# q and k of blocks 6 to 11 turned by transposing transfers instead of TensorE products and ScalarE copies

## The chip, the cores and the metric

The kernel runs on one core of a Trainium2 chip. The metric is the device time of one launch in microseconds, lower is better. Times are of whole launches; a profile is of one launch, recorded by the hardware profiler.

A core has engines that run their own instruction lists in order and wait for each other by semaphores: TensorE (PE in the profile, its weight loads PEld), VectorE (DVE), ScalarE (ACT), GpSimd (POOL) and SyncE (SP). Here GpSimd and SyncE do nothing but issue transfers (DMAs), GpSimd the loads and SyncE the stores. The transfers themselves run on 16 DMA engines that all queues share.

## The reference

Two parts, one behind the other. The first is a recurrence over 768 tokens for 4 batches x 8 heads of 64 dimensions; the second is a channel mix with three matrices.

```python
for t in range(S):                      # per batch and head
    state = gamma * state + outer(k[t], v[t])
    x[t]  = scale * q[t] @ state        # gamma = 1 - 2**(-5-head)
xk = mu_k * x + (1 - mu_k) * x_prev     # x: 4 x 768 x 512, x_prev: one token earlier
xr = mu_r * x + (1 - mu_r) * x_prev
k  = relu(xk @ w_k)                     # 512 x 1024
out = sigmoid(xr @ w_r) * (k * k @ w_v) # 512 x 512, 1024 x 512
```

## The kernel before

The 4 x 768 tokens are cut into 12 blocks of 256 tokens, three to a batch, numbered 0 to 11; a block is two chunks of 128 tokens. The recurrence is done in chunks: scores of k against q inside a chunk, masked by the causal order, times v, plus q times a state that is carried from chunk to chunk. Blocks 6 to 11 (`HALF`) work in four chunks of 64 tokens, so their products are 64x64 on quarters of TensorE's array; blocks 1 to 5 (`WIDE`) use chunks of 128.

There is no scheduler. One list of words, `ORDER` (lines 23 to 74), is walked once, and each word emits its instructions; so each engine's order is the order of its words in that list. A word is a code, a block and further indices; `@` names the PSUM banks that it writes and `~` the engine (v VectorE, a ScalarE, p GpSimd, s SyncE). The words that matter here, for a block n:

- `lq`, `lk`, `lv` (`load`, line 222): GpSimd loads q, k and v. q and k are cast from float32 to float16 on the way, into `Q16` and `K16`, rings of four buffers each. k goes in two transfers, one for each half of the block's 256 tokens (line 230). q goes in one (line 235), with tokens 2p and 2p+1 side by side in partition p.
- `Tq`, `Tk` (`trans`, line 264): TensorE turns q and k, tokens in partitions, into dimensions in partitions, by products with the identity into PSUM; for blocks 6 to 11 these are 32 products of 64x64 each (line 278).
- `Eq`, `Ek` (`turned_q`, `turned_k`): ScalarE copies the turned q and k from PSUM to `QT` and `KT`, rings of three buffers. The copy of q also puts its tokens back into plain order.
- `S` (`scores`, `scores_half`, line 318): TensorE multiplies `KT` with `QT`; `M` (`masked`, line 347): VectorE masks the scores into float16.
- `C`, `U`, `G`: the new state, its sum on VectorE (line 419) and its decay.
- `I` and `J` (`inter`, line 441): TensorE multiplies q with the carried state; `Y` (`intra`, line 462): masked scores with v; `D` (`yout`, line 507): VectorE scales the result into `xT`. For blocks 6 to 11 `Y` ends with the second half of `inter`.
- `dx`, `X` (lines 529 and 538, VectorE): the two mixes xk and xr. `K` (lines 552 and 562), `R` (592) and `V` (604) are TensorE's large products with w_k, w_r and w_v; `Qa`, `Qb` and `s` are ScalarE's relu, square and sigmoid; `O` (line 610, VectorE) multiplies gate and value into `OS`, a ring of four buffers; `st` (line 617) stores it from SyncE.
- `z`: products of zeros that keep TensorE busy early on.

Heads are handled in four pairs, one head in each half of the 128 partitions. `HEADS = ((0, 1), (3, 2), (4, 5), (7, 6))` is the order within the pairs: in two of the four the higher head comes first. `heads(j)` gives for each head of pair j its half `a`, its number and the half `hp` of its output. With this order `inter`, whose products read half `a` and write half `hp`, uses all four 64x64 quarters of the array in turn.

Every transfer has a semaphore out of a ring of eight for GpSimd and of eight for SyncE and ScalarE together, and waits for the transfer that used it last. SyncE's list before is two early loads and 24 stores, each waiting for its `O`.

Of the kernel before, what the change touches and what calls it, by code (L numbers as in the profile page):

```python
# [21 lines left out]
HEADS = ((0, 1), (3, 2), (4, 5), (7, 6))  # L22
ORDER = """
lk.0.0.2~s gy.0 lq.0.2.4~p lv.0~p lq.0.0.2~s lk.0.2.4~p ck.0.0.2~a z.12@6 Tk.0.0.2@0 mu Tq.0.2.4@1
cq.0.0.2~a z.2@6 Tq.0.0.2@2 Ek.0.0.2~a vs.0~v mt@3 Eq.0.0.2~a z.2@6 S.0.1.0.2@45 S.0.0.0.2@67
M.0.0.0.2~v Eq.0.2.4~a M.0.1.0.2~v Tk.0.2.4@2 Ek.0.2.4~a C.0@01 U.0.0~a U.0.1 S.0.0.2.4@67
M.0.0.2.4~v I.0@45 S.0.1.2.4@01 me M.0.1.2.4~v lv.1~p vs.1~v gy.1~a G.0~a z.4@2 Y.0 D.0~v lk.1~p
Tk.1@0 Ek.1~a C.1@67 U.1.0 lq.1~p z.1@2 Tq.1@1 Eq.1~a dx.0~v X.0.0.0 z.4@2 S.1.1@01 lk.2~p I.1@45
S.1.0@23 M.1.1~v M.1.0~v lq.2~p Tq.2@6 Eq.2~a wk.1~p X.0.0.3 Tk.2@0 X.0.0.2 z.1@1 Y.1 J.1 X.0.0.1
D.1~v U.1.1 Ek.2~a z.1@2 S.2.1@01 S.2.0@23 K.0.2@6 dx.1~v K.0.3@4 Qa.0.3 Qa.0.2 wk.0~p z.2@5  # L30
K.0.1@7 Qa.0.1 K.0.0@5 Qb.0.2 X.0.1.0 X.1.0.2 lv.2~p Qa.0.0 Qb.0.1 X.1.0.3 wr~p X.1.0.1 X.1.0.0
K.1.2@4 lv.3~p G.1~a K.1.1@7 X.0.1.1 vs.2~v Qa.1.2 Qb.1.2 M.2.1~v Qb.0.0 C.2@5 U.2.0 K.1.0@6
lq.3~p Qa.1.1 X.0.1.2 X.0.1.3 K.1.3@0 Qa.1.3 I.2@45 R.0.1@1 R.0.0@7 s.0.1 M.2.0~v Y.2 Qa.1.0
X.1.1.3 X.1.1.2 Qb.1.0 Tq.3@1 Eq.3~a J.2 X.1.1.0 X.1.1.1 R.1.0@6 s.0.0 lk.3~p Tk.3@1 vs.3~v D.2~v
dx.2~v X.2.0.2 X.2.0.0 C.3@23 X.2.0.3 Ek.3~a s.1.0 X.2.0.1 lk.4~p U.3.0~a R.1.1@0 lq.4~p s.1.1
Tk.4@1 S.3.1@45 S.3.0@67 Qb.1.1 Qb.1.3 U.3.1 lv.4~p Tq.4@0 Ek.4~a Eq.4~a wv.0~p K.2.2@2 Qa.2.2
M.3.1~v K.2.0@3 Qa.2.0 G.3~a M.3.0~v K.2.3@1 vs.4~v Qb.0.3 S.4.1@45 S.4.0@67 M.4.0~v I.3@23
M.4.1~v Qa.2.3 lq.6~p lq.7~p K.2.1@0 Qb.2.0 Y.3 C.4@67 V.1.0.0@1 U.4.0 U.4.1 G.4~a I.4@45 J.3
# [3 lines left out]
Tq.5@4 Qa.3.1 Qa.3.0 vs.5~v C.5@5 X.2.1.1 Eq.5~a Tk.5@1 Ek.5~a S.6@23 O.0.1 O.1.1 lk.7~p U.5.0  # L42
Tk.7@67 Ek.7~a X.2.1.0 I.5@45 M.6~v X.3.1.3 K.3.2@0 K.3.3@1 Qa.3.2 Qb.3.1 lv.6~p S.5.0@23 Qa.3.3
Qb.3.0 X.3.1.1 S.5.1@67 Qb.3.3 X.2.1.3 Qb.3.2 K.3.4@0 st.0.0 Qa.3.4 M.5.1~v lk.8~p K.3.5@1 Qa.3.5
R.2.1@6 lv.8~p lk.9~p s.2.1 M.5.0~v Y.5 S.7@23 Tk.8@01 Ek.8~a J.5 X.3.1.0 X.3.1.2 R.3.1@7 s.3.1
V.2.0.0@6 K.3.7@0 lv.7~p vs.6~v R.2.0@7 V.2.0.1 D.5~v M.7~v s.2.0 dx.5~v X.5.1.1 O.2.0 Qa.3.7
Qb.3.6 V.2.1.0@1 Tk.9@23 C.6@45 U.6.0~a Ek.9~a lq.8~p Tq.8@67 Qb.3.7 X.5.0.3 V.2.1.1 vs.7~v
R.4.0@0 Eq.8~a U.6.1 U.6.2 X.5.0.0 U.6.3 st.0.1 R.3.0@2 C.7@45 X.5.0.1 s.4.0 I.6@67 s.3.0 st.1.1
X.5.0.2 K.5.3@3 Qa.5.3 O.2.1 lq.10~p K.5.1@0 Qa.5.1 G.6~v X.5.1.3 V.3.0.0@1 U.7.0 U.7.1 U.7.2
st.2.1 I.7@23 Y.6 vs.8~v U.7.3 G.7~a lq.11~p R.4.1@0 D.6~v V.4.1.0@4 lv.11~p C.8@67 Y.7 V.3.1.0@5  # L50
Qb.5.1 Qb.3.4 Qb.3.5 V.3.0.1 dx.6~v s.4.1 U.8.0 U.8.1 V.3.1.1 Qb.5.3 D.7~v U.8.2 V.4.1.1 dx.7~v
X.6.0.1 X.6.0.3 V.4.0.0@7 K.5.0@6 X.5.1.2 X.6.0.2 Qa.5.0 V.4.0.1 Qb.5.0 K.5.2@0 X.6.0.0 Qa.5.2
Qb.5.2 X.6.1.2 lv.9~p K.6.7@6 Qa.6.7 st.2.0 st.1.0 O.4.1 O.3.0 K.6.0@2 Qa.6.0 lk.10~p O.4.0 O.3.1
# [12 lines left out]
V.8.1.0@3 Qb.9.2 X.9.1.0 K.9.0@0 Qa.9.0 Qb.8.2 X.9.1.2 Qb.9.3 K.9.6@1 Qa.9.6 Qb.9.6 O.7.1 st.7.1
K.9.5@7 Qa.9.5 V.8.0.0@0 X.11.0.2 X.11.0.1 Qb.9.0 X.11.0.0 K.11.3@2 K.11.0@1 Qa.11.3 st.6.1
R.8.1@5 V.8.1.1 X.11.1.2 Qa.9.4 st.6.0 X.9.1.3 R.9.1@2 R.10.1@4 R.10.0@6 V.8.0.1 O.8.0 s.8.1
K.11.1@5 Qb.9.4 s.10.0 V.9.0.0@7 V.9.1.0@0 Qa.11.1 Qb.11.1 O.8.1 Qb.9.5 Qb.11.3 Qa.11.0 st.8.1
K.11.2@6 Qa.11.2 V.10.1.0@5 Qb.11.2 Qb.11.0 V.9.1.1 R.9.0@1 X.11.1.3 s.9.0 X.11.1.1 V.9.0.1 O.9.0  # L70
st.9.0 V.11.0.0@6 s.10.1 s.9.1 O.9.1 st.9.1 V.10.0.0@1 V.10.1.1 O.10.1 st.8.0 st.10.1 V.11.0.1
R.11.0@0 s.11.0 O.11.0 V.10.0.1 R.11.1@7 s.11.1 O.10.0 st.10.0 Vc.11.1.1@0 Oc.11.1.1 Vc.11.1.0@6
st.11.0 sc.11.1.1~a Oc.11.1.0 sc.11.1.0~s
# [4 lines left out]
def kernel(  # L78
# [45 lines left out]
    gd_np = gam[np.array(HEADS).T[par // D]] ** TM  # L124
# [16 lines left out]
    Q16 = ring("q16_", 4, [H, 2 * D], F16)  # L141
    K16 = ring("k16_", 4, [H, 2 * D], F16)
# [16 lines left out]
    csm = const.tile([P, 4 * H + (2 + LOG) * NJ + 2 * NCO], F32, name="csm_sb")  # L159
# [14 lines left out]
    gd = csm[:, o : o + NJ]  # L174
# [46 lines left out]

    def load(x, d, split, a=None):
        def go(e, n, j0=0, j1=NJ):
            b, t0 = n // NB, n % NB * TM
            hs = slice(2 * j0, 2 * j1)
            src = x[b, hs, t0 : t0 + TM, :]
            dst = staged(a)[:, hs] if (a, n, j0) in EARLY else d(n)[:, hs]
# [17 lines left out]
    def cast(a):  # L245
        def go(e, n, j0=0, j1=NJ):
            hs = slice(2 * j0, 2 * j1)
            copy(e, (K16 if a else Q16)(n)[:, hs], staged(a)[:, hs])

        return go  # L250
# [13 lines left out]
    def trans(a):  # L264
        def go(e, n, j0=0, j1=NJ):
            pt = turned(n, a, j0)
            src = (K16 if a else Q16)(n)
            for j in range(j0, j1):
                for i in range(2):
                    if whole(n):  # L270
                        for s, h, jo, hp in heads(j):
                            nc.tensor.transpose(  # L272
                                pt[low(s), j, i, :], src[:, h, i * D : i * D + D], ident
                            )
                        continue
                    for u in range(2):
                        for s, h, jo, hp in heads(j):
                            nc.tensor.transpose(
                                pt[low(s), u, j, i, :], src[low(u), h, i * D : i * D + D],
# [25 lines left out]

    def a_half(n):
# [5 lines left out]
    def scores_half(n):  # L312
        pa = banks("S", n).rearrange("p a (j i t) -> p a j i t", j=NJ, i=2)
        for j in range(NJ):
            for i in range(2):
                for a in range(2):
                    for u in range(2):
                        nc.tensor.matmul(  # L318
                            pa[low(u), a, j, i, :], lhsT=KT(n)[low(a), j, i, low(u)],
                            rhs=QT(n)[low(a), j, i, low(u)],  # L320
# [3 lines left out]
    def scores(e, n, i=None, j0=0, j1=NJ):  # L324
# [3 lines left out]
        if wide(n):  # L328
            for j in range(j0, j1):
                for a in range(2):  # L330
                    nc.tensor.matmul(
                        pa[:, a, j, :], lhsT=KT(n)[low(a), j, i, :], rhs=QT(n)[low(a), j, i, :],
# [3 lines left out]
        for j in range(j0, j1):  # L336
            for a in range(2):
                for u in range(2):
                    nc.tensor.matmul(  # L339
                        pa[low(u), a, j, :], lhsT=KT(n)[low(a), j, i, low(u)],  # L340
                        rhs=QT(n)[low(a), j, u, :],
# [17 lines left out]
    def state_half(n):  # L359
        ps = banks("C", n).rearrange("p u (i j d) -> p u i j d", i=2, j=NJ)  # L360
        for j in range(NJ):
            for i in range(2):
                for u in range(2):
                    if more(n) or not (u and i):
                        for a, h, jo, hp in heads(j):
                            nc.tensor.matmul(
                                ps[low(a), u, i, j, :],
                                lhsT=K16(n)[low(u), h, i * D : i * D + D],
# [4 lines left out]
    def state(e, n):  # L373
# [5 lines left out]
        if wide(n):  # L379
            for j in range(NJ):  # L380
                for i in range(2 if more(n) else 1):
                    for a, h, jo, hp in heads(j):
# [3 lines left out]
                            lhsT=K16(n)[:, h, i * D : i * D + D], rhs=VS(n)[:, i, h],  # L386
# [3 lines left out]
        for j in range(NJ):  # L390
            for i in range(2):
                for u in range(2 if more(n) else 1):
                    for a, h, jo, hp in heads(j):
# [3 lines left out]
                            lhsT=K16(n)[low(u), h, i * D : i * D + D],  # L397
# [23 lines left out]
    def decayed(e, n):  # L421
# [342 lines left out]
```

## Time and profile before

| | |
|---|---|
| time before, median of 3 runs | 158.57 us (157.96 to 158.83) |
| profiled execution, span from first to last instruction | 158.7 us |
| TensorE busy | 149.7 us, 2316 matmuls |
| VectorE busy | 128.0 us, 203 operations |
| ScalarE busy | 98.9 us, 182 operations |
| transposing products of blocks 6 to 11 (L278) | 384, first at 49.2 us, last at 108.7 us |
| copies of turned q and k (L241) | 26, of 0.6 to 1.0 us |
| loads issued by GpSimd, last issue | 83.2 us |
| moved by the DMA engines | 22.29 MB in 44903 packets |

The second part of the profile's page cuts the span into 40 slices of 4 us; each digit is the busy share of an engine in tenths. The row of the DMA engines is their mean busy share. In the list of busy times by stage the DMA share can be over 1, as packets of one engine overlap. The list of waits tells which engine stood idle and what ended the wait. The chain is followed back from the last instruction: at each step to what released it, or to the instruction before it on its engine. A timeline's line has the start, the time taken, the engine, the line in the kernel, and what is written and read; several equal instructions are merged, with their number.

### The profile page before, as it was taken

What the parts mean: (1) busy time and instruction counts of PE and PEld (TensorE: products, weight loads), DVE (VectorE), ACT (ScalarE), POOL (GpSimd) and SP (SyncE); (2) the same over time, 40 slices, a digit from 0 to 9 for tenths busy, and PEclk for the clock granted to TensorE, in tenths of its full rate; (3) what the DMA queues carried; (4) which work ended last, traced back from release to release, by engine and by line L of the source; (5) the groups of instructions that cost most, each with busy time, mean ns of one, the idle gap of its engine ahead of it and who ended that gap; (6) DMA issues with size and microseconds to landing.
All of it is one profiled execution on the core that took longest, in us unless ns stands there. A gap on an engine that the chain in (4) does not pass through costs nothing.

```text
span 158.7 us, 5316 instructions
## 1 busy us (share of the span) xinstructions
PE 149.7 (94%) x2316; PEld 85.5 (54%) x2316; DVE 128.0 (81%) x203; ACT 98.9 (62%) x182; POOL 55.1 (35%) x67
## 2 busy tenths in 40 slices
PE   7749989999999999999999999999999999999992
PEld 3334667765765445545654555555565445555451
DVE  2258799999999999999999999999999998040432
ACT  3437452989967479947662689978313498529330
POOL 7999426827967507702992000000000000000000
PEclk9985799999999999999999999999999999999998
DMA  5999999999999999990799934000300015001335
GB/s 151 273 181 175 203 244 243 162 238 182 182 201 179 218 215 175 192 171 9 170 316 216 98 121 150 4 6 0 136 6 4 0 66 197 1 0 70 130 135 198
DMA packets 44903, 22.29 MB, mean 140 GB/s; under 512 B 36424, under 2 KB 40400, under 8 KB 44880
## 3 DMA queue, kind: packets, MB, share of 16 engines
q0 software_dynamic: 39920, 14.95, 73.6%
q1 hardware_dynamic: 4512, 6.69, 11.7%
q10 hardware_dynamic: 448, 0.32, 0.7%
q8 instruction: 18, 0.29, 0.7%
q14 instruction: 5, 0.04, 0.1%
HBM read 24.31 MB, written 6.29 MB: 193 GB/s over the span
## 4 chain that ended last, share of the span: by engine, by line
PE 48%; DVE 31%; DMA 9%; issue 6%; ACT 4%; POOL 0%; DVEq 0%; POOLq 0%
PE ps L604 13%; PE ps L552 9%; PE ps L592 8%; DVE a L354 5%; PE ps L562 5%; DVE xk L538 4%; DVE xr L538 4%; DMA k<-in_k_dram 3%; DVE dx L529 3%; DMA mu<-in_moe_mu_r_dram 3%; DVE vs L253 3%; DVE tg L419 2%; DVE os L610 2%; DVE xT L507 2%; DMA k2s<-in_k_dram 2%
## 5 line engine op out<-in xcount | busy, mean ns | idle before, releaser
L604 PE MATMUL ps<-wv,k2s 128*128 128x512 f16 x184 | 44.4, 380 | 0.0
L571 ACT ACTIVATE kr<-ps 128x512 f32<-128x512 f32 x48 | 27.8, 597 | 21.6 <-PE ps L562 14.6
L604 PEld LDWEIGHTS <-k2s 128*128 128x128 f16 x184 | 17.3, 98 | 18.8
L610 DVE SCALAR_TENSOR_TENSOR os<-ps,rs 128x512 f32<-128x512 f32 x23 | 15.1, 685 | 14.4 <-PE ps L604 7.9
L592 PE MATMUL ps<-wr,xr 128*128 128x512 f16 x96 | 23.9, 380 | 0.0
L230 POOL DMA_DIRECT2D k<-in_k_dram x22 | 19.7, 915 | 12.1 <-PE ps L318 6.6
L562 PE MATMUL ps<-xk,wk 128*128 128x256 f16 x192 | 23.6, 273 | 0.2 <-DVE xk L538 0.2
L552 PE MATMUL ps<-xk,wk 128*128 128x512 f16 x96 | 22.6, 380 | 0.8 <-DVE xk L538 0.8
L598 ACT ACTIVATE rs<-ps 128x512 f32<-128x512 f32 x24 | 14.1, 602 | 13.9 <-PE ps L592 9.8
L230 POOL DMA_DIRECT2D v<-in_v_dram x22 | 19.8, 919 | 8.4 <-DVE vs L253 7.9
L562 PEld LDWEIGHTS <-wk 128*128 128x128 f16 x192 | 18.2, 98 | 4.8 <-DVE xk L538 0.5
L538 DVE SCALAR_TENSOR_TENSOR xr<-dx,mu,xT 128x256 f16<-128x256 f32 (+1 forms) x36 | 19.4, 569 | 0.0
L538 DVE SCALAR_TENSOR_TENSOR xk<-dx,mu,xT 128x256 f16<-128x256 f32 (+1 forms) x36 | 18.8, 568 | 0.2
L241 ACT COPY kT<-ps 128x1024 f16<-128x1024 f16 (+1 forms) x13 | 12.2, 951 | 9.3 <-PE ps L272 5.9
L253 DVE TENSOR_TENSOR vs<-v,csm_sb 128x1024 f16<-128x1024 f32 x12 | 14.6, 1219 | 3.1 <-DMA v<-in_v_dram 3.1
L354 DVE TENSOR_TENSOR a<-ps,c_sb 128x1024 f16<-128x1024 f32 (+1 forms) x14 | 14.4, 1067 | 1.9 <-PE ps L339 1.5
L552 PEld LDWEIGHTS <-wk 128*128 128x128 f16 x96 | 9.0, 98 | 12.1 <-DVE xk L538 1.1
L583 ACT ACTIVATE k2s<-kr 128x512 f16<-128x512 f32 x24 | 14.8, 632 | 0.2
L529 DVE TENSOR_TENSOR dx<-xT 128x1024 f32<-128x1024 f32 x12 | 14.7, 1222 | 0.2
L579 ACT ACTIVATE k2s<-kr 128x512 f16<-128x512 f32 x24 | 14.7, 628 | 0.1
L241 ACT COPY qT<-ps 128x1024 f16<-128x1024 f16 (+1 forms) x13 | 12.3, 952 | 3.5 <-PE ps L272 3.4
L592 PEld LDWEIGHTS <-xr 128*128 128x128 f16 x96 | 8.7, 98 | 9.7
(67 smaller groups left out, 157.8 us busy)
## 6 DMA issues: line engine op xcount, KB each, us to landing
out_dram<-os SPq DMA_DIRECT2D x23, 256.0 KB, 2.4
v<-in_v_dram POOLq DMA_DIRECT2D x22, 256.0 KB, 7.2
k<-in_k_dram POOLq DMA_DIRECT2D x23, 128.0 KB, 7.0
q<-in_q_dram POOLq DMA_DIRECT2D x11, 256.0 KB, 7.7
wk<-in_moe_w_k_dram POOLq DMA_DIRECT2D x2, 512.0 KB, 10.9
wv<-in_moe_w_v_dram POOLq DMA_DIRECT2D x2, 512.0 KB, 8.0
v<-in_v_dram POOLq DMA_DIRECT2D x1, 512.0 KB, 6.2
wr<-in_moe_w_r_dram POOLq DMA_DIRECT2D x1, 512.0 KB, 13.2
```

The source lines that it names most:

```text
L230: e.dma_start(out=dst[:, :, i * D : i * D + D], in_=src[:, i * P : i * P + P].rearrange("h p d -> p h d"),)
L241: e.copy(out=out, in_=in_)
L253: e.tensor_tensor(out=VS(n), in0=V32(n).rearrange("p h (i d) -> p i h d", i=2), in1=gks[:, int(half(n) or wide(n)), :, :, None].to_broadca ...
L354: nc.vector.tensor_tensor(out=a_full(n)[:, i, :, j0:j1], in0=pairs(banks("S", n, i, j0))[:, :, j0:j1], in1=(below if wide(n) else causal[: ...
L529: e.tensor_tensor(out=DX(k)[:, :, m * TM + t0 : m * TM + t1], in0=x[:, :, c + t0 : c + t1], in1=x[:, :, c - 1 + t0 : c - 1 + t1], op=ALU.s ...
L538: nc.vector.scalar_tensor_tensor(out=XM[w](k)[:, j, t0:t1], in0=DX(k)[:, j, t0:t1], scalar=mu[:, w * NCO + j : w * NCO + j + 1], in1=x[:, ...
L552: nc.tensor.matmul(banks("K", n, g), lhsT=wk16[:, co, g * P : g * P + P], rhs=XM[0](k)[:, co, :], start=(co == 0), stop=(co == NCO - 1),)
L562: nc.tensor.matmul(pz[:, i, :], lhsT=wk16[:, co, fo * P : fo * P + P], rhs=XM[0](k)[:, co, m * TM + t0 : m * TM + t1], start=(i == 0 and c ...
L571: nc.scalar.activation(out=kr, in_=banks("K", n, g, *u), func=AF.Relu)
L592: nc.tensor.matmul(banks("R", n, tb), lhsT=XM[1](k)[:, co, t : t + P], rhs=wr16[:, co, :], start=(co == 0), stop=(co == NCO - 1),)
L604: nc.tensor.matmul(banks("V", n, tb), lhsT=K2(n)[:, fo, tb * P : tb * P + P], rhs=wv16[:, fo, :], start=(fo == 0), stop=(fo == NFO - 1),)
L610: nc.vector.scalar_tensor_tensor(out=OS(2 * n + tb), in0=banks("V", n, tb), scalar=1.0 / (KSC * KSC), in1=RS(2 * n + tb), op0=ALU.mult, op ...
```

## The change

For blocks 6 to 11 (`SIDE`) the words `Tq`, `Tk`, `Eq` and `Ek` are gone. Twelve words `tq` and `tk` on SyncE's queue stand in the list where `Eq` and `Ek` stood; a single product of zeros (`z.1`) takes the place of the `Tq` of block 7. Each issues one transposing transfer of 128 x 1024 float16 values from `Q16` or `K16` straight to `QT` or `KT`. Nothing else moves in the list.

For these transfers q and k of the blocks lie in another order in `Q16` and `K16` (first both halves of the tokens, then heads), so that q too is loaded by two transfers, one for each half. A transposing transfer can't put one head of a pair into the other half, so blocks 6 to 11 (batches 2 and 3, `PLAINB`) use the pairs in plain order, with their own decay constants. `inter` then writes half `a` only, and two of the four accumulation areas of a block are begun by `intra` instead.

```diff
+PLAIN = ((0, 1), (2, 3), (4, 5), (6, 7))
+SIDE = (6, 7, 8, 9, 10, 11)
+PLAINB = (2, 3)
...
-Qa.2.1 D.3~v dx.3~v Y.4 V.1.1.0@6 Tq.7@23 J.4 D.4~v wv.1~p Qb.2.1 V.0.1.0@0 lk.6~p V.0.0.0@7
-X.2.1.2 dx.4~v X.3.0.1 X.3.0.2 X.3.0.3 Eq.7~a V.1.1.1 X.3.0.0 V.0.0.1 O.0.0 Tk.6@45 Ek.6~a lq.5~p
-Tq.6@23 lv.5~p Qb.2.2 V.0.1.1 Eq.6~a V.1.0.1 O.1.0 K.3.6@4 K.3.1@5 Qb.2.3 lk.5~p K.3.0@7 Qa.3.6
+G.4~a I.4@45 J.3 Qa.2.1 D.3~v dx.3~v Y.4 V.1.1.0@6 z.1@2 J.4 D.4~v wv.1~p Qb.2.1 V.0.1.0@0
+lk.6~p V.0.0.0@7 X.2.1.2 dx.4~v X.3.0.1 X.3.0.2 X.3.0.3 tq.7~s V.1.1.1 X.3.0.0 V.0.0.1 O.0.0
+tk.6~s lq.5~p lv.5~p Qb.2.2 V.0.1.1 tq.6~s V.1.0.1 O.1.0 K.3.6@4 K.3.1@5 Qb.2.3 lk.5~p K.3.0@7
...
-    def heads(j):
-        return [(a, h, h // 2, h % 2) for a, h in enumerate(HEADS[j])]
+    def heads(j, n):
+        return [(a, h, h // 2, h % 2) for a, h in enumerate((PLAIN if n // NB in PLAINB else HEADS)[j])]
...
     def load(x, d, split, a=None):
...
+            if a is not None and side(n):
+                dst = d(n).rearrange("p (i h d) -> p i h d", i=2, h=H)
+                for i in range(2):
+                    e.dma_start(out=dst[:, i], in_=src[:, i * P : i * P + P].rearrange("h p d -> p h d"))
+                return
...
+    def flipped(a):
+        def go(e, n):
+            e.dma_start_transpose(
+                out=(KT if a else QT)(n).rearrange("c j i p -> c (j i) p"), in_=(K16 if a else Q16)(n)
+            )
+
+        return go
+
+    def tposed(a, n, s, j, i):
+        t = (KT if a else QT)(n)
+        if side(n):
+            return t.rearrange("c j i p -> c (j i) p")[low(s), i * NJ + j, :]
+        return t[low(s), j, i, :]
...
     def intra_half(n):
         py = pairs(banks("I", n))
+        fresh = [n // NB in PLAINB] * 2
...
+                        begin = hp == u and fresh[u]
+                        if begin:
+                            fresh[u] = False
...
-                            start=False, stop=False, skip_group_check=True,
+                            start=begin, stop=False, skip_group_check=True,
```

SyncE's list in the changed kernel, in order: the two early loads; q7, k6, q6, k7; store 0.0; k8, k9, q8; stores 0.1, 1.1, 2.1, 2.0, 1.0, 3.1; k10, q10, q11, q9; stores 3.0, 4.1; k11; the other stores. On TensorE 384 products and their weight loads are gone and one product of zeros is added; on ScalarE 12 copies are gone; GpSimd issues six more loads; VectorE's list is the same.

More of the change, by code (lines that the diff above doesn't have):

```diff
@@ new lines @@
+vs.8~v U.7.3 G.7~a lq.11~p R.4.1@0 D.6~v V.4.1.0@4 lv.11~p C.8@67 Y.7 V.3.1.0@5 Qb.5.1 Qb.3.4
+Qb.3.5 V.3.0.1 dx.6~v s.4.1 U.8.0 U.8.1 V.3.1.1 Qb.5.3 D.7~v U.8.2 V.4.1.1 dx.7~v X.6.0.1
+X.6.0.3 V.4.0.0@7 K.5.0@6 X.5.1.2 X.6.0.2 Qa.5.0 V.4.0.1 Qb.5.0 K.5.2@0 X.6.0.0 Qa.5.2 Qb.5.2
+X.6.1.2 lv.9~p K.6.7@6 Qa.6.7 st.2.0 st.1.0 O.4.1 O.3.0 K.6.0@2 Qa.6.0 lk.10~p O.4.0 O.3.1
+st.3.1 K.6.4@0 S.8@67 I.8@23 Qa.6.4 K.6.1@1 tk.10~s X.6.1.1 X.5.1.0 Qa.6.1 Qb.6.1 K.6.6@0 Qb.6.0
+Qa.6.6 vs.9~v K.6.5@4 Qa.6.5 M.8~v R.5.1@1 Qb.6.6 tq.10~s s.5.1 Y.8 Qb.6.7 lv.10~p vs.10~v
@@ new lines @@
+X.6.1.3 tq.11~s D.8~v dx.8~v lq.9~p X.8.0.2 X.8.0.1 lk.11~p R.5.0@0 s.5.0 K.6.3@6 Qa.6.3
+V.5.1.0@7 X.6.1.0 tq.9~s S.10@45 M.10~v Qb.6.3 C.9@01 U.9.0~v st.3.0 U.9.1 V.5.1.1 K.6.2@6
+Qa.6.2 R.6.1@2 s.6.1 U.9.2 R.6.0@3 s.6.0 I.9@45 U.9.3 O.5.1 X.8.0.3 S.9@01 M.9~v X.8.0.0 G.9~a
+C.10@67 U.10.0 U.10.1 Qb.6.2 vs.11~v R.7.1@2 s.7.1 V.5.0.0@3 Qb.6.5 st.4.1 tk.11~s U.10.2 U.10.3
+V.5.0.1 Qb.6.4 K.8.0@2 Qa.8.0 G.10~v I.10@01 Y.9 C.11@67 st.4.0 R.7.0@2 O.5.0 V.6.1.0@3 D.9~v
+U.11.0 U.11.1 s.7.0 K.8.3@4 Qa.8.3 V.6.1.1 U.11.2 I.11@67 st.5.0 dx.9~v O.6.1 S.11@45 X.8.1.2
@@ new lines @@
+X.11.1.2 Qa.9.4 st.6.0 X.9.1.3 R.9.1@2 R.10.1@4 R.10.0@6 V.8.0.1 O.8.0 s.8.1 K.11.1@5 Qb.9.4
+s.10.0 V.9.0.0@7 V.9.1.0@0 Qa.11.1 Qb.11.1 O.8.1 Qb.9.5 Qb.11.3 Qa.11.0 st.8.1 K.11.2@6 Qa.11.2
+V.10.1.0@5 Qb.11.2 Qb.11.0 V.9.1.1 R.9.0@1 X.11.1.3 s.9.0 X.11.1.1 V.9.0.1 O.9.0 st.9.0
+V.11.0.0@6 s.10.1 s.9.1 O.9.1 st.9.1 V.10.0.0@1 V.10.1.1 O.10.1 st.8.0 st.10.1 V.11.0.1 R.11.0@0
+s.11.0 O.11.0 V.10.0.1 R.11.1@7 s.11.1 O.10.0 st.10.0 Vc.11.1.1@0 Oc.11.1.1 Vc.11.1.0@6 st.11.0
+sc.11.1.1~a Oc.11.1.0 sc.11.1.0~s
@@ L123 @@
     h_pj = 2 * np.arange(NJ)[None, :] + (par // D)[:, None]
-    gd_np = gam[np.array(HEADS).T[par // D]] ** TM
+    gd_np = np.concatenate([gam[np.array(x).T[par // D]] ** TM for x in (HEADS, PLAIN)], axis=1)
     g0_np = 0.125 * KSC / KUP * gam[h_pj] ** (1 - TM)
@@ L195, in low, with side, natural @@
         return slice(a * D, a * D + D)
-    def heads(j):
-        return [(a, h, h // 2, h % 2) for a, h in enumerate(HEADS[j])]
+    def heads(j, n):
+        return [(a, h, h // 2, h % 2) for a, h in enumerate((PLAIN if n // NB in PLAINB else HEADS)[j])]
+    def side(n):
+        return n in SIDE
+    def natural(t, n, h, i):
+        if side(n):
+            return t[:, i * H * D + h * D : i * H * D + h * D + D]
+        return t[:, h * 2 * D + i * D : h * 2 * D + i * D + D]
     def half(n):
@@ L270, in go @@
                     if whole(n):
-                        for s, h, jo, hp in heads(j):
+                        for s, h, jo, hp in heads(j, n):
                             nc.tensor.transpose(
-                                pt[low(s), j, i, :], src[:, h, i * D : i * D + D], ident
+                                pt[low(s), j, i, :], natural(src, n, h, i), ident
                             )
@@ L276, in go @@
                     for u in range(2):
-                        for s, h, jo, hp in heads(j):
+                        for s, h, jo, hp in heads(j, n):
                             nc.tensor.transpose(
-                                pt[low(s), u, j, i, :], src[low(u), h, i * D : i * D + D],
+                                pt[low(s), u, j, i, :], natural(src, n, h, i)[low(u)],
                                 ident[low(u), low(u)],
@@ L364, in state_half @@
                     if more(n) or not (u and i):
-                        for a, h, jo, hp in heads(j):
+                        for a, h, jo, hp in heads(j, n):
                             nc.tensor.matmul(
                                 ps[low(a), u, i, j, :],
-                                lhsT=K16(n)[low(u), h, i * D : i * D + D],
+                                lhsT=natural(K16(n), n, h, i)[low(u)],
                                 rhs=VS(n)[low(u), i, h],
@@ L381, in state @@
                 for i in range(2 if more(n) else 1):
-                    for a, h, jo, hp in heads(j):
+                    for a, h, jo, hp in heads(j, n):
                         o = ps[low(a)]
@@ L392, in state @@
                 for u in range(2 if more(n) else 1):
-                    for a, h, jo, hp in heads(j):
+                    for a, h, jo, hp in heads(j, n):
                         o = ps[low(a)]
@@ L437, in inter @@
             for i in range(parts):
-                for a, h, jo, hp in heads(j):
+                for a, h, jo, hp in heads(j, n):
                     u = a ^ s
@@ L460, in intra_half @@
                 for u in range(2):
-                    for a, h, jo, hp in heads(j):
+                    for a, h, jo, hp in heads(j, n):
+                        begin = hp == u and fresh[u]
+                        if begin:
+                            fresh[u] = False
                         nc.tensor.matmul(
@@ L476, in intra @@
                 for i in range(2):
-                    for a, h, jo, hp in heads(j):
+                    for a, h, jo, hp in heads(j, n):
                         nc.tensor.matmul(
@@ L487, in intra @@
                 for u in range(2):
-                    for a, h, jo, hp in heads(j):
+                    for a, h, jo, hp in heads(j, n):
                         nc.tensor.matmul(
```

109 lines of the change are left out of this document (48 added, 61 removed).

## The prediction

> **What bounds the kernel now.** I read the page's busy rows first, then the busy times by stage, then the waits of each engine, then the chain that ended last, and at the end the timelines of TensorE, VectorE and the DMA issues around the twelve places that the change touches.
>
> ```profile
> PE 149.7 (94%) x2316; PEld 85.5 (54%) x2316; DVE 128.0 (81%) x203; ACT 98.9 (62%) x182; POOL 55.1 (35%) x67
> ...
> PE   7749989999999999999999999999999999999992
> ...
> DVE  2258799999999999999999999999999998040432
> ACT  3437452989967479947662689978313498529330
> ...
> DMA  5999999999999999990799934000300015001335
> ```
>
> Two engines, not one, are full from slice 7 to slice 32; ScalarE is not. By stages (columns: PE, PEld, DVE, ACT, POOL busy us, then clock, DMA share, GB/s):
>
> ```profile
> 50.00:70.00 20.00, 19.84 (x350) 10.28 (x349) 19.86 (x27) 14.70 (x23) 9.72 (x11) 1.00 1.40 194
> 70.00:90.00 20.00, 19.77 (x364) 11.17 (x361) 19.48 (x35) 11.39 (x23) 9.71 (x11) 1.00 1.08 171
> 90.00:110.00 20.00, 19.71 (x467) 10.42 (x468) 19.42 (x30) 17.83 (x32) 0.00 (x0) 1.00 0.17 57
> 110.00:124.00 14.00, 13.61 (x295) 8.30 (x293) 13.58 (x23) 4.03 (x8) 0.00 (x0) 1.00 0.12 42
> ```
>
> Which of the two sets the pace is told by who waits. The list of waits of VectorE for the stretch 49 to 124 us is empty: no gap there is longer than 0.13 us, and those that are there stand before operations that read PSUM. TensorE does wait for VectorE, five times, 0.14 to 0.40 us. The chain says the same at its last change of engine:
>
> ```profile
> 118.60 0.70 DVE xT L507
> ...
> 119.33 1.24 DVE dx L529
> ...
> 120.59 2.75 DVE xk L538 x4
> ...
> 123.39 1.89 PE ps L552 x8
> ```
>
> VectorE works without a pause until 123.3 us, TensorE then takes K.9, which had to wait 0.40 us for xk, and runs 32.2 us of matmuls without a gap to 155.6 us. So the end is VectorE's path to 123.3 plus that tail. The change has no VectorE instruction in it, and none of TensorE's that lies behind 123.4.
>
> **The change part by part.**
> 1. *Removed from TensorE:* twelve groups of 32 transposing products (L278), six blocks times q and k. In the timeline a group takes 0.27 us of TensorE's stream, from its start to the start of what follows:
>
> ```profile
> 49.22 0.45 PE L278 MATMUL ps<-c_sb,q 64*64 64x64 f16 x32
> 49.49 0.28 PE L441 MATMUL ps<-qT,tg 64*64 64x128 f16 x8
> ```
>
> 12 x 0.27 = 3.2 us, less one filler product (0.22 us, a 128x512 product at the 0.86 us of four): 3.0 us. All twelve lie between 49 and 109 us, where VectorE has no wait that they could shorten. I cost them at nothing: TensorE would arrive 3.0 us early at K.9 and wait there for xk. At most the four or five gaps of 0.1 us go, 0.4 us.
> 2. *Removed from ScalarE:* twelve copies of 1.01 us, 12.1 us. ScalarE idles 2 to 9 us in each of the stages of 20 above, and in the empty list no VectorE operation waits for it. Nothing.
> 3. *Plain head pairs:* inter (L441) then uses two of the four 64x64 quarters of the array for a block instead of four. A group of 16 takes 0.15 us now (97.72 to 97.88); if two quarters halve its rate it takes 0.30: 11 groups, 1.7 us at most, 0 at least. It is covered by the 3.0 us that TensorE has won. Nothing.
> 4. *Loads of q split in two:* six more issues on GpSimd at 0.92 us. For blocks 6 and 7 they fall before GpSimd's idle 6.65 us ahead of 60.4 us, for 8, 10 and 11 before its 7.87 us ahead of 74.5 us. Those loads land up to 0.9 us later for each split before them; q of block 8 is the one that matters (below). Block 9's split delays only k of block 11, whose scores come last.
> 5. *Added: twelve transposing transfers of 256 KB on SyncE's queue.* No such transfer is in the trace. From below, the nearest row is the store of 256 KB on the same queue: 2.0 us from issue to landing when the DMA engines are quiet (128.7 us), 3.9 us for the one at 56.5 us and 5.9 us for the third of those at 77 us, under the loads. From above, the packets: the page has
>
> ```profile
> q0 software_dynamic: 39920, 14.95, 73.6%
> ```
>
> 73.6% of 16 x 158.7 us over 39920 packets is 47 ns of an engine for a packet of 375 B. If a transfer goes as 1024 pieces of 256 B (a row of one 128x128 square in fp16), that is 1024 x 47 ns / 16 = 3.0 us of all engines; at 128 B a piece and the 66 ns of a q1 packet (11.7% over 4512), 8.4 us; at 32 B and 47 ns, 24 us. These are estimates; the piece is not shown. I take 3.0 us for each in a row, behind a first landing of 5.9 us under load or 5.0 (2.0 + 3.0) in the quiet stretch, the lowest of the three upper prices, since v loads of 256 KB in 1024 pieces of 256 B land 1.1 to 1.5 us apart in this trace, nearer to it than the other two are.
>
> The Trainium skill, page "DMA: Bandwidth & Descriptors", section "Latency and other measured facts", has 261 GB/s for transposing transfers; with a fixed 2 us from its section "Anatomy of one DMA", 256 KB would land in an estimated 3 us. By it none of the waits below would arise and the sum would be 158.6; no run here shows it so far.
>
> Now who waits. TensorE takes its instructions in order, so a late transfer holds all that stands behind the first scores that read it, and the masking of those scores (M) stands in VectorE's order:
>
> ```profile
> 59.80 0.44 PE L318 MATMUL ps<-qT,kT 64*64 64x64 f16 x32
> ...
> 105.47 0.32 PE L441 MATMUL ps<-qT,tg 64*64 64x64 f16 x12
> 105.62 0.50 PE L318 MATMUL ps<-qT,kT 64*64 64x64 f16 x32
> ```
> ```profile
> 60.47 1.22 DVE L347 TENSOR_TENSOR a<-ps,c_sb 128x1024 f16<-128x1024 f32 x1
> ...
> 106.54 1.22 DVE L347 TENSOR_TENSOR a<-ps,c_sb 128x1024 f16<-128x1024 f32 x1
> ```
>
> - *S.6 at 59.80.* The first three transfers (q7, k6, q6) can't go before J.4 has freed the buffer that q7 writes, at 49.8 us; the stage 48 to 56 has a DMA share of 1.87. Landings at 49.8 + 5.9 = 55.7, then 58.7 and 61.7. S.6 is 1.9 us late; its products end 60.24 and M.6 begins 60.47, 0.2 us of cover. **+1.7 us**.
> - *Store 0.1.* It stands on SyncE behind the transfer of q8, and so behind the landing of q8 (69.3, with the split and the two k transfers on the wire about 71.7). It would land near 78 instead of 61.4. O.2.1 writes that buffer at 76.41, by now 78.1. Nothing, but the cover is gone: each further us of delay is a us of VectorE.
> - *S.10 and I.9.* k10 stands behind store 3.1 (93.2): landings 98.6 and, for q10, 101.6. S.10 is at 101.25, M.10 at 102.63: covered. q11 waits for J.8 (97.9), lands 104.6; q9 lands 107.6. I.9 reads it at 105.47: 2.1 us late; S.9 then ends 0.4 us ahead of M.9 (106.54) as it is now. **+1.7 us**.
> - S.7, S.8 and S.11 have their operands 1.5 us or more ahead by the same count.
>
> Sum: 1.7 + 1.7 = 3.4 us on the profiled execution's 158.7 us (its span; the runs' median is 158.57, 0.1 us less): 162.1 us, and against the median **162.0 us**.
>
> **The rivals.**
> - *A, in time.* A transfer takes the store's 2.0 to 3.9 us. Three then land by 59 us and nothing waits: VectorE's path stands, 158.2 to 159.4 us. For it: same queue, same bytes as the stores. Against it: DMA engines are at a share of 1.87 where the first three go.
> - *B, heavier transfers.* At 6 us each in a row S.6 is 7.9 us late and I.9 14.1 us (landings from 93.6 + 8 us): 180 us; at 8.4 us, past 190. An idle TensorE also loses clock: here it was busy 2.16 of the 5 us from 5 us on, and the granted clock was 0.60 and 0.72 in the next two stretches of 5 us. For it: no row shows the price, and SyncE's queue is one. Against it: the loads do 1024 pieces in 1.1 to 1.5 us.
>  The Trainium skill, page "VectorE: DVE Perf Modes", section "The three transpose paths", gives 1309 ns for one 128x128 square by DMA; if the eight squares of a transfer went one behind the other, that is an estimated 10.5 us and this rival, past 190 us. No run here shows it so far.
> - *C, faster.* If VectorE's full row hides slack (its ends overlap the next start by 0.09 us, so a short wait can be lost), TensorE's 3.0 us count in full: 155.7 us, or 157.4 if part 3 costs its most. It decides if VectorE's path before 123.3 us shortens by over 0.8 us. Against it: the empty list of waits.
>
> **How the numbers follow.** A measurement tells 0.5% (0.8 us) from no change. Forecast (159.4 to 168): 0.39. A: 0.27, within 0.5%. B to 180: 0.15; B above: 0.12. C: 0.07. Faster 0.07, same 0.27, slower 0.66. The range runs from 158.0 (A with the 0.4 us of gaps and the median's 0.1) to 180 and leaves out C and the far end of B, 0.19.
>
> **What would show it.** Right: the transfers of k6 and q6 land after 59.8 us, TensorE's S.6 and VectorE's M.6 wait for them, and again near 105 us; VectorE has no other new wait; TensorE waits over 2 us for xk ahead of K.9. Wrong: landings under 4 us (A), a run of landings over 5 us apart (B), K.9 starting before 122.5 us (C), or waits at places that I gave cover: O.2.1 on store 0.1, S.10.

## The result and the profile after

The changed kernel takes 170.28 us (median of four runs, 168.45 to 171.74); the kernel before, on the same chip, 158.7 us (157.96 to 160.46). The ratio is 1.073 (95% interval 1.063 to 1.082): slower by some 11.6 us. The kernel before runs some 3 us longer when TensorE gets half its clock early on (157.55 us at a mean granted clock of 1.00, 160.14 to 160.64 us at 0.976 to 0.978, on the chip of the first experiments); the medians here take in both kinds of run, the ratios the faster alone. The two profiled executions, which the following compares, both have that early stretch and differ by a little less: a span of 167.9 us against 158.7 us, 9.2 us.

The page of the changed kernel, in the rows that the prediction showed of before:

```profile
PE 150.1 (89%) x1933; PEld 84.7 (50%) x1933; DVE 128.6 (77%) x203; ACT 88.2 (53%) x170; POOL 60.4 (36%) x73
...
PE   7759989999999720999999999998999999999990
...
DVE  2366799999999940799999999999999999040441
...
PEclk9995799999999995699999999999999999999999
...
q0 software_dynamic: 46160, 14.95, 78.0%
q1 hardware_dynamic: 17184, 9.83, 28.0%
```

The clock of the kernel before, which the prediction did not show:

```profile
PEclk9985799999999999999999999999999999999998
```

PE and DVE, full from slice 7 on before, now have one hole, at slices 14 and 15, counted from 0 (59 to 67 us; a slice is 4.2 us). The clock of slices 15 and 16 is 0.5 and 0.6, where before it was full. Behind them both rows are as full as they were. ScalarE has 10.7 us less to do, VectorE as much as before.

From the list of waits for 49 to 132 us (total, times, longest), the four of TensorE and VectorE over 0.5 us; VectorE had none before:

```profile
PE ps L352 <- DMA qT<-q: 7.0, 1, 7.0
DVE a L381 <- PE ps L352: 7.0, 1, 7.0
PE ps L591 <- DVE xk L577: 0.9, 1, 0.9
DVE a L388 <- PE ps L365: 0.8, 1, 0.8
```

The first line is S.6 (L352 now): TensorE stood for q of block 6. The second is M.6 behind it. The third stands at 56.1 us, ahead of K.3, and not at K.9. The last is M.5: the eight products of K ahead of its scores ran at half clock and took 3.00 us. No transfer is waited for at S.10 or I.9. The chain of waits has the same place as its longest piece (start, us):

```profile
56.18 10.79 DMA qT<-q
66.97 0.04 issue
67.01 0.65 PE ps L352 x20
```

The transfer of q6 was issued at 56.18 us and landed at 66.97. SyncE's timeline shows why it was issued so late; the second column is the time that SyncE needed to issue one transfer:

```profile
49.99 1.35 SPq L328 DMA_TRANSPOSE qT<-q  x1
51.44 4.63 SPq L328 DMA_TRANSPOSE kT<-k  x1
56.18 3.33 SPq L328 DMA_TRANSPOSE qT<-q  x1
59.61 6.14 SPq L328 DMA_TRANSPOSE kT<-k  x1
```

A store under the loads took 0.3 to 0.5 us to issue in the kernel before. Under the loads, q7, k6, q6 and k7 landed at 59.59, 66.19, 66.97 and 71.67 us, 9.6 to 14.8 us after their issue. In the quiet stretch from 100 to 116 us the same transfers are another thing (the last number is the median from issue to landing):

```profile
qT<-q SPq DMA_TRANSPOSE x3, 3.1
kT<-k SPq DMA_TRANSPOSE x2, 4.5
```

There an issue took 1.24 to 1.44 us. The account: M.6 begins at 67.70 instead of 60.47 us (7.2 late); the half clock adds 0.8 at M.5; some 0.3 is spread behind it; K.9 begins at 131.74 instead of 123.39 (8.35 late). From K.9 to VectorE's last operation both kernels take the same 32.2 us, and 0.8 us more pass after it, up to the end of the span.

### The profile page after: what moved, and what is told of

Same layout as the page of the kernel before. It is cut to its first block, busy times and chain, and to the rows that moved or that the text cites. A ratio compares the mean times of both kernels' runs of the same rounds, so it can differ in the third digit from the quotient of the medians.

```text
span 167.9 us, 4579 instructions
## 1 busy us (share of the span) xinstructions
PE 150.1 (89%) x1933; PEld 84.7 (50%) x1933; DVE 128.6 (77%) x203; ACT 88.2 (53%) x170; POOL 60.4 (36%) x73
## 4 chain that ended last, share of the span: by engine, by line
DVE 33%; PE 27%; DMA 25%; issue 8%; POOL 4%; ACT 1%; DVEq 0%; POOLq 0%
DMA k<-in_k_dram 9%; PE ps L643 8%; DMA qT<-q 6%; PE ps L591 6%; DMA q<-in_q_dram 5%; DVE xk L577 4%; PE ps L631 4%; DVE xT L546 4%; DVE dx L568 4%; DVE vs L273 4%; DVE tg L453 3%; DVE os L649 3%; DVE a L388 3%; DVE xr L577 3%; DMA mu<-in_moe_mu_r_dram 3%
## 5 line engine op out<-in xcount | busy, mean ns | idle before, releaser
L591 PE MATMUL ps<-xk,wk 128*128 128x512 f16 x96 | 23.7, 393 | 1.2 <-DVE xk L577 0.9
L637 ACT ACTIVATE rs<-ps 128x512 f32<-128x512 f32 x24 | 14.1, 597 | 17.5 <-PE ps L631 11.2
L245 POOL DMA_DIRECT2D k<-in_k_dram x12 | 10.7, 905 | 7.1 <-PE ps L292 5.4
L381 DVE TENSOR_TENSOR a<-ps,c_sb 128x1024 f16<-128x1024 f32 x6 | 7.3, 1217 | 7.0 <-PE ps L352 7.0
L245 POOL DMA_DIRECT2D q<-in_q_dram x12 | 10.7, 901 | 5.4 <-PE ps L292 2.2
```

Of the source, the lines that this page charges most:

```text
L245: e.dma_start(out=dst[:, i], in_=src[:, i * P : i * P + P].rearrange("h p d -> p h d"))
L591: nc.tensor.matmul(banks("K", n, g), lhsT=wk16[:, co, g * P : g * P + P], rhs=XM[0](k)[:, co, :], start=(co == 0), stop=(co == NCO - 1),)
```

## The experiments

Twelve kernels. The theories: the loss is the wait for the first transfers, made long by transposing beside the loads; against it, that small pieces do it, turned or not; that the plain pairs, the split loads or the order on SyncE do it; or that the loss is spread over all blocks. Where a block goes back to products, its words `Tq`, `Tk`, `Eq` and `Ek` stand in the list again; the cuts of code leave that out.

**Parts of the change alone.** Four kernels beside the kernel before (160.26 us, 157.55 to 160.64, on that chip). Plain head pairs, with products and copies as before:

```diff
-SIDE = (6, 7, 8, 9, 10, 11)
+SIDE = ()
 PLAINB = (2, 3)
```

> Blocks 6 to 11 with plain head pairs and with the kernel before's products, copies and loads: no transfer turns anything. Theory (late under load: the whole loss is the 7 us that S.6 waits for q of block 6, whose transfer is late because it shares the DMA engines with the loads): 158.7 us within 0.5, VectorE without a wait from 49 to 123 us, though inter may take up to 0.15 us more a group. Rival (plain pairs): if half of the array's quarters slow inter enough to be late for VectorE, 160 us or more, with waits of VectorE on L441-type products.

Measured 160.5 us (160.15 to 162.29): no change. Counted in the timeline, the 176 products of inter from 70 us on take 3.4 us of TensorE's stream instead of 2.3; no loss shows, though TensorE has won nothing in this kernel.

The transfers of blocks 10 and 11 alone:

```diff
-SIDE = (6, 7, 8, 9, 10, 11)
+SIDE = (10, 11)
-PLAINB = (2, 3)
+PLAINB = (3,)
```

> Only blocks 10 and 11 by transposing transfers (q and k, four transfers, all issued after 93 us, when the DMA engines are quiet). Theory: each lands 3 to 4.5 us after its issue, no wait on TensorE or VectorE, 158.7 us within 0.5. Rival (a transposing transfer is slow by itself, some 10 us each): k10 and q10 land near 113 us, S.10 waits some 10 us, 168 us.

Measured 160.68 us (160.38 to 162.08): no change, and no wait on a transfer; they landed 3.2 to 4.9 us after issue.

Those of blocks 6 and 7 alone:

```diff
-SIDE = (6, 7, 8, 9, 10, 11)
+SIDE = (6, 7)
-PLAINB = (2, 3)
+PLAINB = (2,)
```

> Only blocks 6 and 7 by transposing transfers (four transfers, issued from 50 us on, while the loads run). Theory: q6 lands near 67 us as in the changed kernel, S.6 waits some 7 us, and nearly the whole loss is there: 167 to 170 us. Rival (the loss is spread over all twelve, by more packets and later stores): 161 to 164 us, S.6's wait well under 7 us.

Measured 169.16 us (166.38 to 172.19): 8.9 us over the kernel before, most of the loss, with a wait of 9.2 us at S.6 and one of 1.8 us at M.5. Four transfers of twelve hold it. The wait is longer than 7.0 us since this trace has no half clock early on: TensorE comes to S.6 2.8 us earlier, at 57.2 us, while q6 lands at 66.42 us, nearly as in the changed kernel.

All twelve transfers as plain copies of the same 256 KB, at the same places; q and k of blocks 6 to 11 are then not turned:

```diff
-            e.dma_start_transpose(
-                out=(KT if a else QT)(n).rearrange("c j i p -> c (j i) p"), in_=(K16 if a else Q16)(n)
+            e.dma_start(
+                out=(KT if a else QT)(n).rearrange("c j i p -> c (j i p)"), in_=(K16 if a else Q16)(n)
             )
```

> The changed kernel with each transposing transfer replaced by a plain copy of the same 256 KB between the same buffers, so q and k of these blocks are not turned (the output leaves the turning out). Theory (the transposing transfer's 1056 small packets share the engines packet by packet with the loads): a copy has 128 rows of 2 KB, lands in 4 to 6 us as the stores do under load, q6 by 58 to 60 us, S.6 waits 0 to 1 us: 158.5 to 160 us. Rival (any further 256 KB on SyncE's queue at that time is as late): S.6 waits 5 to 7 us, 165 to 170 us.

Measured 160.81 us (159.76 to 161.65): no wait at S.6, and at most some 2 us more. From `dx` of block 3 to the end of VectorE's last operation its trace takes 107.0 us, as before (115.2 in the changed kernel); behind that the span ends 0.8 us later, as in the changed kernel. So neither the bytes, nor the places on SyncE's queue, nor the split loads of q make the loss. The issues between 49 and 62 us in its trace:

```profile
qT<-q SPq DMA_DIRECT2D x2, 256.0 KB, 7.7
kT<-k SPq DMA_DIRECT2D x2, 256.0 KB, 7.5
```

A plain copy needs 7.5 to 7.7 us under these loads and 0.5 to 0.6 us to issue, and that is in time; the changed kernel's row for the same stretch has 10.2 for q and 13.4 for k.

**Small pieces or turning.** The transfers as ordinary copies that read 256 B at a time from four places of a partition (two copies of 128 KB for each transfer; again nothing is turned):

```diff
-            e.dma_start_transpose(
-                out=(KT if a else QT)(n).rearrange("c j i p -> c (j i) p"), in_=(K16 if a else Q16)(n)
-            )
+            for i in range(2):
+                e.dma_start(
+                    out=(KT if a else QT)(n).rearrange("c j i p -> c (j i p)")[
+                        :, i * NJ * C : (i + 1) * NJ * C
+                    ].rearrange("c (j p) -> c j p", j=NJ),
+                    in_=(K16 if a else Q16)(n).rearrange("p (j i d) -> p j i d", j=NJ, i=2)[:, :, i],
+                )
```

> Each transposing transfer becomes two ordinary copies of 128 KB that read pieces of 256 B from four places of a partition (the q and k of blocks 6 to 11 are then not turned: their scores and states are of other data). Same bytes and about the same number of pieces as the transposing transfer (1024 of 256 B), same places in SyncE's order; only the turning is gone. Theory (turning itself is what is slow beside the loads): the copies land within 9 us of their issue as the plain copies with long pieces did (7.3 to 7.9 us), no wait of TensorE at S.6 over 0.5 us, time 159 to 162 us. Rival (small pieces are slow beside the loads, turned or not): S.6 waits 4 us or more, time 165 us or more.

Measured 165.83 us (165.05 to 166.73), ratio 1.044 (1.032 to 1.057), with 3.4 us of wait at S.6. The time is in the range of the second theory, the wait between the two, each of which said that the other's part was nothing. The DMA rows for 54 to 64 us (packets, MB, share of 16 engines) tell the two apart. The changed kernel:

```profile
q0 software_dynamic: 2229, 0.71, 109.2%
q1 hardware_dynamic: 1950, 0.49, 59.1%
```

The small copies:

```profile
q0 software_dynamic: 3530, 1.06, 86.9%
q1 hardware_dynamic: 3897, 0.97, 57.3%
```

And transposing transfers with nothing beside them, in the kernel with blocks 10 and 11 alone, 95 to 97 us:

```profile
q1 hardware_dynamic: 1566, 0.39, 103.5%
```

Alone, the transfers get 783 packets per us, 196 GB/s. Small copies and loads together get 743, 204 GB/s: they share, and 1024 pieces have to take their turn. Transposing transfers and loads together get 418, 121 GB/s (plain copies and loads 251 GB/s): here the rate itself breaks down, most of all from 60 to 64 us, at 205 packets per us. In the packets of the stretch, size by size, the mean time is about double that beside the small copies: a load's 128 B took 59 ns instead of 32, its 4 KB 481 instead of 218, a piece of 256 B 48 instead of 24. So small pieces delay the first scores by some 3 us, and turning doubles that. The two issues for each transfer make this split rough.

**Order.** k6 and q6 ahead of q7, since S.6 reads them first; the loads that must stand ahead of them move up too:

```diff
-... I.4@45 J.3 Qa.2.1 ... D.4~v wv.1~p Qb.2.1 V.0.1.0@0 lk.6~p ... tq.7~s ... tk.6~s ... tq.6~s
+... I.4@45 wv.1~p lk.6~p J.3 tk.6~s tq.6~s Qa.2.1 ... D.4~v Qb.2.1 V.0.1.0@0 ... tq.7~s ...
```

> The changed kernel with one reordering: k6 and q6 go ahead of q7 on SyncE's queue and right behind J.3 (their words, and those of the loads of k6 and of half of w_v that must stand before them, move up; GpSimd's order stays). They can go at about 47.8 us instead of 51.4 and 56.2. Theory (S.6 waits for q6's landing; under load the first lands some 10 to 11 us after its issue and the next 3.7 us later): k6 lands near 58, q6 near 62 us, S.6 waits some 2 us instead of 7.0: span 160 to 162 us. Rival (the DMA engines have no room for the transfers before the loads let up, at about 66 us): q6 lands at 65 to 67 us as before the reordering, S.6 waits 5 to 7 us, 165 to 168 us.

Measured 178.47 us (177.37 to 179.64; before, on that chip, 157.46), ratio 1.130 (1.118 to 1.142): worse. q6 was issued 6.4 us earlier, at 49.75 us, and landed only 3.7 us earlier, at 63.27: S.6 still waited 5.5 us. And a second wait appeared on VectorE:

```profile
92.14 0.69 DVE L647 SCALAR_TENSOR_TENSOR os<-ps,rs 128x512 f32<-128x512 f32 x1 [9.06 <-DMA out_dram<-os]
```

That is O.2.1 on store 0.1, which stands behind the transfer of q8, the place where the prediction said that the cover is gone. In the changed kernel it landed at 84.53 us and O.2.1 began at 84.63.

Loads k8 and v8 behind k9 and v7, so that fewer loads lie beside the first transfers, and stores 0.1 and 1.1 ahead of k8:

```diff
-M.5.1~v lk.8~p K.3.5@1 Qa.3.5 R.2.1@6 lv.8~p lk.9~p s.2.1 M.5.0~v Y.5 S.7@23 tk.8~s
+M.5.1~v K.3.5@1 Qa.3.5 lk.9~p lv.7~p lk.8~p lv.8~p R.2.1@6 s.2.1 M.5.0~v Y.5 S.7@23 st.0.1 st.1.1 tk.8~s
```

> The changed kernel with the loads of k and v of block 8 moved behind those of k9 and v7 in GpSimd's order, which wait for a buffer until about 60 us, so that no load is issued between about 50 and 60 us; and stores 0.1 and 1.1 moved ahead of k8 on SyncE's queue, so that they don't wait for it. q7, k6 and q6 stay where they are. Theory (the transfers are late because they share the engines with the loads): with the loads gone by 56 us k6 lands by 58 and q6 by 60 to 62 us, S.6 waits 0 to 2 us; span 158.5 to 161.5 us, if v7 and v8 are not late for VectorE. Rival (SyncE's issue, 4.6 us for k6, is the limit by itself): q6 goes at 56 us again and lands at 65 us or later, S.6 waits 5 to 7 us.

Measured 169.09 us (168.01 to 170.29), ratio 1.068 (1.053 to 1.083): no gain. This trace too has no half clock early on, so the early transfers go some 3.5 us sooner than in the changed kernel. S.6 waited 8.8 us for q6 all the same, and the loads of k7, now beside the first transfers, landed at 59.8 and 62.8 us instead of 53.7 and 54.6: an ordinary load was slowed too. Fewer loads behind the first transfers hardly made these faster. Nor does an earlier issue: q6 was issued at 56.18 us in the changed kernel, at 52.86 with blocks 6 and 7 alone, 52.42 here and 52.81 in the next kernel, and landed at 66.97, 66.42, 65.39 and 67.33 us.

The scores read later, S.6 and M.6 where S.7 and M.7 stood, those where the turning of k9 stood, and the stores ahead:

```diff
-Ek.5~a S.6@23 ... M.6~v ... S.7@23 tk.8~s ... M.7~v ... V.2.1.0@1 C.6@45
+Ek.5~a ... S.6@23 st.0.1 st.1.1 tk.8~s ... M.6~v ... V.2.1.0@1 S.7@23 C.6@45 ... M.7~v
```

> The full change, with S.6 and M.6 moved to where S.7 and M.7 stood (66.3 and 69.2 us before the change), S.7 and M.7 to where the turning of k9 stood (72.3 us), and the stores of rows 0 and 1 of the second half put ahead of k8 on SyncE. Theory (the loss is the wait of the first scores, not work or traffic as such): q6, landing near 67 us as in the changed kernel, is then late by 1 us at most, k7 by less than 1 us; 158 to 163 us. Rival (the slowed transfers and loads hold up something else, v of blocks 6 and 7 or the buffers): another wait of 4 us or more on VectorE or TensorE between 60 and 90 us, 165 us or more.

Measured 175.37 us (171.43 to 176.95; before 160.49): the rival, in the profiled execution (171.43 us, the fastest) too. S.6 still waited, and others came:

```profile
PE ps L398 <- DVE tg L451: 5.6, 1, 5.6
DVE vs L271 <- DMA v<-in_v_dram: 5.3, 2, 5.1
PE ps L350 <- DMA qT<-q: 3.8, 1, 3.8
DVE xT L551 <- PE ps L474: 2.5, 1, 2.5
```

The second line is mostly the scaling of v of block 7: its load landed at 81.55 us, in the kernel before at 68.27. In the changed kernel that load landed at 72.47, 4.2 us late, and was read at 81.11 us, 8.2 us later than before, behind the wait at S.6; at the old time, 72.96 us, it would have been in time by 0.5 us. Here it was issued 2.2 us later than there and took 16.6 us instead of 9.8; what made that load so slow was not settled. With the scores later in the list, the loads' own delay shows: the loss is not one wait that this place could hide.

**Without the costly four.** Transfers for blocks 8 to 11 alone:

```diff
-SIDE = (6, 7, 8, 9, 10, 11)
+SIDE = (8, 9, 10, 11)
```

> Blocks 8 to 11 by transposing transfers (eight), blocks 6 and 7 by products and copies as before, all with plain pairs. k8, k9 and q8 still go while the loads run, but their readers come 20 us later. Theory (only the wait of S.6 costs): those three land 10 us or more after their issue and nobody waits for them; the same as before within 0.5%, at most some tenths from store 0.1 behind q8. Rival (transfers under load also cost by holding up the loads and the stores behind them): VectorE waits for v of block 7 or, at O.2.1, for store 0.1, 1 to 4 us, 160 to 163 us on the profile's span.

Measured 160.73 us (158.4 to 162.19 in nine runs of ten; before 157.46), ratio 1.014 (1.010 to 1.019). The tenth, of 500.38 us, is the profiled one, so where the 2 us went was not seen. The same with stores 0.1 and 1.1 ahead of k8:

```diff
 SIDE = (8, 9, 10, 11)
-... S.7@23 tk.8~s ... U.6.3 st.0.1 R.3.0@2 ... s.3.0 st.1.1
+... S.7@23 st.0.1 st.1.1 tk.8~s ... U.6.3 R.3.0@2 ... s.3.0
```

> Transposing transfers for blocks 8 to 11 alone, and the stores of rows 0 and 1 of the second half ahead of k8 on SyncE. Theory (what blocks 8 to 11 alone cost, some 2 us, was the store that stood behind q8): within 0.8 us of the kernel before, and no wait for the output buffer on VectorE. Rival (k8, k9 and q8 slow the loads, or the plain pairs cost): still 1.5 us or more above, with the wait at another place. TensorE's saving of 8 x 0.27 = 2.2 us shows nowhere, as VectorE has no pause to give up.

Measured 160.56 us (157.7 to 163.12; before 160.49), ratio 0.995 (0.988 to 1.002): no change, no wait of VectorE from 49 to 130 us, no gap of TensorE over 0.41 us. That fits the store as the cause in the kernel without the move, but with no trace of that one it is not shown. Eight turnings less on TensorE gain nothing either.

**Does TensorE's saving pay if VectorE is relieved?** Both with the scaling of v of blocks 9 to 11 on GpSimd; the first without transfers (its text says plain pairs; the kernel has the pairs of before), the second with those of blocks 8 to 11:

```diff
-vs.9~v ... vs.10~v ... vs.11~v
+lk.11~p vs.9~p vs.10~p ... vs.11~p
```

> The kernel before (products and copies for all blocks, plain pairs), with the scaling of v of blocks 9, 10 and 11 moved from VectorE to GpSimd, behind its last loads of k. VectorE has 3 x 1.14 = 3.4 us less to do before K.9. Theory (VectorE and TensorE are both full until 123 us, so that relief of one alone gains only what the other's gaps hold, some 0.9 us in all): 0 to 0.6% faster. Rival (VectorE alone sets the pace): 2% faster. If GpSimd's scaling takes over 5 us each, the states of block 9 wait for it and the time rises.

> Transposing transfers for blocks 8 to 11 alone, the stores of rows 0 and 1 of the second half ahead of k8, and the scaling of v of blocks 9, 10 and 11 on GpSimd. Theory (the transfers do relieve TensorE by 8 x 0.27 = 2.2 us, and this pays as soon as VectorE is relieved too): 2 to 3 us (1.2 to 1.9%) faster than the kernel before, about 2 us faster than the same move without the transfers. Rival (the transfers beside the loads of 60 to 72 us cost as much as they save, or the scaling on GpSimd is late): no faster than the other kernel of this pair.

Measured 161.7 us (158.22 to 163.66; before 157.51), ratio 1.007 (1.002 to 1.012), and 161.65 us (160.1 to 164.41), ratio 1.023 (1.016 to 1.030): both slower, the second against theory and by more. The relief was none. VectorE's line of two xk products, in the kernel before and then in the second of these:

```profile
86.95 1.42 DVE L538 SCALAR_TENSOR_TENSOR xk<-dx,mu,xT 128x512 f16<-128x512 f32 x2
```
```profile
87.20 4.58 DVE L575 SCALAR_TENSOR_TENSOR xk<-dx,mu,xT 128x512 f16<-128x512 f32 x2
```

Beside it, on GpSimd:

```profile
86.76 2.16 POOL L271 TENSOR_TENSOR vs<-v,csm_sb 128x1024 f16<-128x1024 f32 x1
89.13 2.10 POOL L271 TENSOR_TENSOR vs<-v,csm_sb 128x1024 f16<-128x1024 f32 x1 [0.21 <-DMA v<-in_v_dram]
```

While GpSimd scaled, VectorE's two products stood: 3.2 us lost, for 2.3 us taken from it by these two scalings. TensorE then waited 3.1 us for xk. So the question stays open; what is known is its size: 3.0 us of products less 1.1 us for the plain pairs, 1.9 us at most, for all six blocks.

No version of these beats the kernel before.

## Why the prediction was wrong

The sign and the first place were right: a transfer late at S.6. The sum was 3.4 us and the loss 11.6. By its own steps:

- *Products, copies, plain pairs and split loads of q at nothing:* right as to the time. No wait of VectorE closed, and the tail from K.9 is the same 32.2 us. But TensorE did not arrive 3.0 us early at K.9: it waited 0.15 us there for xk (0.40 before) and not over 2. From S.6 to K.9 its stream lost 2.8 us of turning products, but inter took 5.2 us of it instead of 2.7, in part for plain pairs (1.1 us in the kernel with these alone), and the products of K 20.0 instead of 18.9, by the half clock.
- *The piece of 256 B:* right. The changed kernel's first DMA queue of hardware descriptors has 12672 packets more, 12 x 1056, and 12288 of them have 256 B.
- *3.0 us for each in a row, behind a first landing of 5.9 us under load:* **this is the step that failed**, by the size of its terms. Both prices came from other kinds of transfer, a store and v loads, that had been seen beside each other; nothing in the trace showed how a transposing transfer and loads share. The first landing took 9.6 us instead of 5.9, the two behind it 7.4 us instead of 6.0 (6.6 and 0.8), so that the third came 17.2 us after J.4 had freed the buffer instead of 11.9. S.6: 7.0 us instead of 1.7. The row that decided for 3.0 us was also misread: in the trace of before the v loads went as 64 packets of 4 KB each and not as 1024 pieces; the loads that do go in 1024 packets (k, 128 B each) landed 0.6 to 1.3 us apart, so the price would have been no higher by them. SyncE's issue, 1.35 to 6.14 us each, was not costed at all, but issuing q6 3.3 to 3.8 us earlier brought its landing forward by 1.6 us at most. The runs with plain copies and with small copies show that this is not the place, the queue or the bytes: small pieces make part, turning beside loads the rest.
- *I.9 at 1.7 us:* wrong the other way, 0. In the quiet stretch the landing was 3.1 to 4.5 us, under the 5.0 taken, and an issue each 1.3 us.
- *Half clock after a long idle:* named under rival B, not in the sum; 0.8 us.
- *Store 0.1, cover gone:* right. It landed 0.1 us ahead of O.2.1, both some 6.5 us later than forecast; that the margin came out the same is luck. With k6 and q6 first it became a wait of 9.06 us.
- *Span against median:* wrong by the time around a span. Every run here takes 1.7 to 2.0 us more than its span, so the profiled execution of before, 158.7 us of span, is the run of 160.46 us, 1.8 us above the median of 158.7; that of the changed kernel, 169.63 us, is 0.65 us below its own. Together these are the 2.4 us between 9.2 and 11.6. The forecast of 162.0 is the median and 3.4 us and does not hang on it.

Rival B, 6 us each in a row, had S.6 7.9 us late, close to the 7.0 measured, and the time in its range; but its second term (I.9, 14.1 us) was nothing, as the transfers are heavy only beside loads. So neither price held for the whole kernel: the forecast's was too high for the quiet stretch and B's too low for the first landing.

The estimate of 3 us from the Trainium skill (page "DMA: Bandwidth & Descriptors", sections "Latency and other measured facts" and "Anatomy of one DMA") agrees with the quiet landings of q, 3.1 us, not with that of k, 4.5 us, and not with those under load, 9.6 to 14.8 us; the second section's 2 us are those of a transfer that GpSimd issues. The one from the Trainium skill, page "VectorE: DVE Perf Modes", section "The three transpose paths", 10.5 us for eight squares, does not agree: eight squares landed in 3.1 us.

## What to carry to other kernels

Price a transfer by a row that was taken beside the same traffic; where no such row exists, let the unknown rate, not only the unknown size, set the upper end. Check in the trace, and not in the code, in what pieces the transfer of that row went. Moving work from a full engine to the DMA engines can pay only if that engine alone sets the pace; here VectorE was as full, and the late transfers were free and useless, while the four early ones by themselves cost some 9 us. Before hiding a wait, look which loads come due next: they may be late too.

## What the hardware showed that was not expected

- Transposing transfers beside GpSimd's loads: 418 packets per us in all from 54 to 64 us (205 from 60 to 64), against 783 for the transfers alone and 743 for small ordinary copies beside the same loads. Most of the packets keep their time; a few take much more (in the changed kernel, 60 to 64 us, one load packet in twenty over 0.95 us). What holds them is not in the trace, and was not settled.
- In the changed kernel SyncE's issue of a transposing transfer took 1.24 to 1.44 us in quiet, up to 6.14 us under load; that of a store mostly 0.3 to 0.6.
- TensorE had no product from 60.0 to 67.0 us; the granted clock was 0.50 from 63.3 to 70.1 us, the last three with TensorE at work again.
- VectorE's operation with two operands in SBUF stood while GpSimd's scaling ran (4.58 us for 1.42). The Trainium skill, page "SBUF — State Buffer", section "SBUF: two separate sides", says that such an operation and one of GpSimd that reads SBUF exclude each other for a whole instruction; the trace agrees.
